# Block 1 of a long convolution: two of four spectra kept as halves, rows 0 and 2 summed first, h loaded in two transfers, new orders

## The chip, the cores and the metric

The kernel runs on one core of one Trainium2 chip. The metric is the device time of one execution in microseconds. Times inside a profile are microseconds from the start of its span.

## The reference

Two layers follow each other, twice over, on x with 2048 positions and 512 channels in bf16. The first is a gated long convolution, the second a feed-forward network (FFN):

```
kv = shift_conv4(k, shift_k) * v
y  = irfft(rfft(pad(kv)) * rfft(pad(ssm_k)))[:2048] + kv * ssm_D
x  = x + layernorm(x) * y
x  = x + (silu(n @ w_gate) * (n @ w_up)) @ w_down     # n = layernorm(x), F = 1792
```

The convolution's y depends on k, v and the filter alone, and not on x; both passes use the same y.

## The kernel before

**Blocks.** The 2048 positions are cut into 4 blocks of 512 (`NB`). A block is held as four rows of 128 positions (position = 4p + r, row r), and its transform has length 1024. The convolution is done block by block: spectra X of kv and G of the filter h, products of X of block i with G of block j summed into Z of block i + j, and one inverse transform for each block of y. The transforms are matmuls with tables of cosines and sines: `fwd`, made on ScalarE from angles, and `inv`, its transpose, made by two DMA transposes (L1158) on SP's queue.

**Spectra of the first block.** All spectra consist of four slots of a real and an imaginary part, 128 partitions by 512 channels each. With a, b, c, d for the partial transforms over two rows each, slot 0 is a + c, slot 2 is a - c, slot 1 is b + d, slot 3 is b - d. `half` (L425) makes partial transforms with two matmuls a part; `butterfly` (L437) adds and subtracts them on VectorE (DVE); `direct` (L450) makes a slot with four matmuls a part and needs no butterfly. Before, G of block 0 is made by `half` and `butterfly`, X of block 0 by `direct` in all four slots. ScalarE (ACT) copies the results out of PSUM (L419), DVE some of them (L422).

**Products and inverse.** `product` (L627) multiplies one slot: two multiplications of 1024 columns (L642) and two combinations of 512 (L646). `inverse_half` (L783) forms z0 + z2, z0 - z2, z1 + z3 and z1 - z3 (L791) and makes each row of y with four matmuls (L797): rows 0 and 2 from the sums, rows 1 and 3 from the differences.

**Units.** The FFN works through units of two rows (a layer, a block, rows 0 and 2 or rows 1 and 3). The first unit takes rows 0 and 2 of block 0. `prologue` (L879) makes its input: DVE multiplies the normalised x with y straight from PSUM (L903, the tile n), adds it to x (L908), takes statistics (L809), GpSimd (POOL) forms rstd (L814), DVE normalises to z (L864), TensorE (PE) transposes z (L920), and a copy by ACT and one by DVE (L925, L923) give zT, from which the first FFN matmuls (L311, tile pf) read. In a unit, gate and up projections fill PSUM, ACT copies them (L970, L974), DVE multiplies them to ht (L977), and the down projection (L990) adds up in the tile pd.

**Loads.** SP issues, in this order: h of block 0 (hn), k of block 0 (kn), v (vt) and x (xc) of block 0, h and v of block 1, the gate weights, the two table transposes, k of block 1, the up and down weights. PE turns h by 16 transposes (L477), k by another 16 (L366), and makes the short convolution with diagonal matrices dg (L1152) in 64 matmuls of 128 columns; `shift_mul` (L497) then multiplies with v on DVE (L524).

**Order.** Every operation is recorded first (`Plan.add`) with its engine, a planned cost, and what it reads and writes. `ORDER` is a written list that gives each recorded operation its place; `Plan.order` sorts by it and assigns buffers from rings, and `Plan.issue` puts out the instructions in that order, so each engine's queue is fixed. Where the plan sees PE idle for more than 0.5 us in the first 32 us, `issue` puts in warming matmuls (tile wm, L1267), whose results nobody reads; their operand wz is set by DVE (L1050).

Of the kernel before, what the change touches and what calls it, by code (L numbers as in the profile page):

```python
# [9 lines left out]
P = 128  # L10
# [22 lines left out]
X0 = 'direct'  # L33
# [9 lines left out]
H_SPLIT = False  # L43
# [7 lines left out]
LASTV = True  # L51
ORDER = [
    0, 8, 122, 2, 4, 5, 12, 9, 3, 6, 1, 31, 32, 33, 10, 14, 7, 11, 15, 16, 18, 21, 17, 20, 22, 23, 36, 30, 56, 73, 153, 24, 40, 25, 41, 34, 42, 38,
    55, 54, 68, 50, 64, 58, 62, 71, 81, 13, 26, 77, 48, 28, 43, 29, 27, 53, 35, 49, 37, 57, 65, 52, 47, 69, 51, 19, 39, 60, 66, 67, 61, 63, 44, 45,
    154, 155, 156, 196, 258, 197, 83, 84, 85, 86, 88, 80, 90, 91, 92, 94, 78, 96, 97, 98, 103, 79, 99, 100, 101, 108, 76, 89, 93, 107, 95, 123, 145,
    171, 147, 176, 159, 87, 82, 114, 115, 121, 105, 111, 113, 102, 104, 46, 59, 70, 75, 72, 74, 118, 109, 106, 110, 112, 116, 117, 126, 131, 136, 140,
    124, 125, 133, 139, 148, 151, 144, 150, 157, 128, 120, 132, 129, 119, 130, 137, 141, 142, 134, 146, 163, 152, 158, 177, 164, 127, 135, 138, 149,
    160, 168, 199, 213, 167, 183, 189, 202, 170, 209, 165, 175, 187, 200, 162, 172, 143, 185, 161, 173, 166, 169, 207, 208, 204, 205, 178, 181, 179,
    180, 225, 226, 182, 184, 206, 212, 234, 192, 215, 186, 198, 190, 193, 195, 194, 201, 210, 211, 216, 217, 227, 230, 233, 221, 228, 235, 237, 229,
    238, 239, 246, 252, 260, 270, 263, 271, 264, 291, 292, 294, 296, 293, 295, 299, 300, 309, 314, 334, 310, 311, 244, 243, 272, 275, 262, 245, 277,  # L60
    276, 203, 222, 232, 188, 214, 218, 174, 191, 219, 236, 254, 285, 257, 281, 320, 321, 231, 241, 223, 224, 273, 286, 315, 317, 305, 307, 289, 301,
    335, 333, 347, 345, 363, 354, 220, 261, 290, 368, 283, 282, 313, 324, 323, 342, 379, 365, 380, 416, 425, 429, 432, 437, 445, 444, 478, 471, 524,
    515, 479, 522, 540, 551, 504, 512, 548, 573, 611, 547, 627, 644, 639, 649, 250, 251, 253, 259, 256, 268, 247, 248, 284, 302, 316, 240, 242, 278,
    279, 269, 274, 280, 288, 306, 322, 327, 266, 298, 249, 255, 287, 297, 265, 267, 318, 331, 328, 308, 319, 312, 325, 330, 336, 338, 337, 339, 340,
    341, 344, 353, 358, 352, 357, 346, 350, 364, 370, 390, 366, 369, 355, 385, 381, 392, 402, 407, 408, 414, 421, 367, 375, 388, 389, 398, 406, 356,
    411, 413, 427, 428, 409, 418, 410, 422, 426, 431, 430, 438, 439, 440, 348, 351, 359, 360, 361, 362, 373, 377, 376, 382, 378, 384, 393, 394, 396,
    395, 397, 401, 404, 412, 420, 446, 417, 443, 441, 452, 451, 453, 454, 466, 483, 482, 486, 487, 488, 499, 492, 497, 500, 507, 510, 527, 508, 536,
    462, 467, 473, 481, 447, 455, 485, 494, 495, 520, 519, 460, 461, 449, 450, 469, 470, 456, 457, 503, 523, 526, 496, 511, 513, 514, 477, 506, 490,
    509, 518, 566, 531, 528, 530, 468, 484, 533, 594, 579, 618, 598, 619, 655, 640, 436, 343, 463, 464, 489, 493, 498, 501, 525, 532, 537, 539, 543,
    538, 541, 544, 546, 559, 564, 567, 572, 304, 400, 383, 475, 476, 491, 505, 549, 574, 586, 587, 591, 589, 601, 608, 614, 660, 672, 675, 729, 332,  # L70
    329, 303, 326, 371, 349, 374, 386, 405, 415, 419, 424, 372, 399, 474, 480, 423, 472, 458, 459, 434, 442, 387, 403, 529, 552, 558, 599, 593, 624,
    669, 648, 542, 535, 502, 433, 517, 516, 521, 448, 569, 534, 545, 575, 560, 576, 435, 465, 555, 581, 582, 595, 606, 609, 628, 625, 631, 641, 643,
    673, 688, 626, 636, 658, 659, 653, 654, 686, 690, 632, 650, 670, 678, 721, 704, 794, 796, 772, 748, 719, 391, 863, 738, 683, 652, 684, 697, 702,
    715, 722, 723, 802, 808, 814, 815, 817, 835, 839, 845, 886, 847, 887, 888, 891, 893, 896, 900, 911, 912, 899, 901, 915, 916, 894, 924, 925, 939,
    941, 950, 957, 955, 958, 972, 979, 1010, 1018, 1044, 565, 570, 580, 588, 577, 583, 578, 590, 592, 613, 621, 561, 568, 550, 556, 553, 563, 554,
    557, 571, 623, 667, 562, 585, 604, 605, 597, 602, 596, 600, 607, 645, 674, 629, 638, 584, 620, 646, 656, 679, 657, 687, 691, 705, 707, 603, 616,
    617, 633, 615, 634, 610, 622, 637, 709, 713, 630, 681, 651, 676, 665, 668, 642, 671, 694, 710, 714, 689, 699, 677, 680, 696, 701, 685, 698, 708,
    717, 716, 693, 700, 682, 692, 706, 718, 724, 720, 725, 726, 730, 731, 737, 739, 761, 762, 752, 755, 785, 798, 792, 734, 767, 768, 769, 758, 759,
    744, 745, 776, 799, 793, 773, 780, 746, 751, 775, 783, 756, 757, 795, 801, 807, 781, 800, 779, 806, 809, 812, 810, 813, 811, 825, 727, 732, 728,
    733, 736, 743, 749, 753, 754, 763, 764, 766, 765, 770, 771, 786, 787, 791, 816, 788, 789, 826, 831, 829, 832, 833, 841, 842, 843, 848, 849, 855,  # L80
    862, 865, 866, 870, 876, 878, 882, 884, 913, 898, 917, 834, 836, 820, 823, 837, 840, 818, 838, 850, 881, 874, 856, 858, 819, 824, 854, 857, 852,
    853, 875, 889, 890, 844, 869, 846, 851, 860, 871, 864, 872, 879, 909, 892, 885, 895, 828, 830, 897, 964, 921, 965, 922, 968, 1013, 1046, 742, 735,
    747, 790, 777, 867, 868, 877, 880, 902, 903, 904, 907, 905, 906, 908, 932, 933, 956, 982, 943, 976, 740, 741, 784, 804, 859, 861, 883, 914, 910,
    937, 945, 974, 961, 981, 990, 996, 998, 1002, 1029, 1030, 1015, 1032, 635, 647, 661, 612, 662, 663, 666, 664, 778, 822, 712, 750, 703, 711, 695,
    760, 805, 821, 774, 782, 797, 803, 827, 873, 993, 992, 1009, 999, 1008, 1006, 1058, 1020, 983, 1024, 971, 1031, 926, 1007, 952, 985, 1036, 967,
    975, 1011, 1052, 1057, 1047, 1056, 1037, 1049, 1060, 1079, 1063, 1106, 1098, 1101, 1135, 1110, 1112, 1109, 1120, 1132, 1137, 1177, 1179, 1161,
    1183, 1182, 1188, 1146, 1147, 1163, 1165, 1192, 1194, 1195, 1212, 1210, 1213, 1108, 1066, 1061, 1069, 1092, 1153, 1157, 1158, 1159, 1214, 1226,
    1235, 1240, 1254, 1247, 1255, 1264, 1265, 1268, 1274, 1273, 1293, 1289, 1279, 1283, 1294, 1320, 1276, 1278, 1305, 1313, 938, 940, 935, 936, 944,
    948, 947, 953, 954, 986, 977, 920, 923, 927, 928, 918, 919, 931, 934, 942, 987, 978, 960, 966, 929, 930, 951, 963, 969, 970, 973, 995, 1005, 946,
    959, 949, 962, 980, 997, 1016, 1035, 1022, 1043, 1072, 1071, 984, 988, 1027, 1028, 1004, 1012, 1014, 1021, 1041, 1054, 1059, 1000, 1019, 989,  # L90
    1001, 1003, 1017, 991, 994, 1025, 1074, 1064, 1040, 1048, 1033, 1045, 1042, 1051, 1023, 1026, 1053, 1075, 1065, 1034, 1038, 1039, 1050, 1055,
    1076, 1067, 1077, 1068, 1083, 1062, 1070, 1073, 1082, 1102, 1113, 1097, 1103, 1124, 1133, 1136, 1090, 1091, 1078, 1080, 1081, 1087, 1086, 1089,
    1096, 1134, 1143, 1114, 1131, 1104, 1105, 1125, 1130, 1095, 1100, 1149, 1150, 1154, 1111, 1115, 1121, 1122, 1140, 1151, 1160, 1156, 1162, 1166,
    1084, 1088, 1085, 1093, 1094, 1099, 1116, 1107, 1117, 1118, 1127, 1128, 1119, 1126, 1129, 1144, 1148, 1152, 1145, 1164, 1168, 1170, 1167, 1169,
    1171, 1172, 1173, 1185, 1190, 1191, 1198, 1200, 1202, 1204, 1206, 1207, 1208, 1220, 1221, 1223, 1236, 1189, 1199, 1181, 1184, 1174, 1176, 1175,
    1196, 1209, 1216, 1218, 1187, 1201, 1186, 1193, 1203, 1205, 1197, 1224, 1225, 1234, 1233, 1217, 1222, 1178, 1180, 1211, 1229, 1215, 1219, 1230,
    1241, 1238, 1227, 1239, 1228, 1237, 1253, 1262, 1277, 1270, 1284, 1329, 1366, 1462, 1123, 1138, 1141, 1142, 1155, 1231, 1232, 1246, 1242, 1258,
    1252, 1297, 1299, 1302, 1303, 1306, 1307, 1308, 1309, 1310, 1312, 1311, 1321, 1139, 1269, 1324, 1325, 1326, 1327, 1334, 1335, 1336, 1338, 1339,
# [140 lines left out]
def kernel(  # L239
# [936 lines left out]
    else:  # L1176
# [22 lines left out]
        elif X0 == "direct":  # L1199
            direct(vt[0], X[0], "pf", eng(XVE[2:]), (2, 1, 3))  # L1200
# [100 lines left out]
```

## Time and profile before

| what | us |
|---|---|
| runs | 344.19, 344.80, 345.65 (median 344.8) |
| the profiled execution, and its span | 344.93, 343.2 |
| busy in the span: PE, DVE, ACT, POOL | 336.4, 283.4, 253.9, 35.3 |
| first matmul; h turned; first matmul of the v spectrum | 1.04; 4.49 to 6.35; 14.62 |
| v products of block 0 on DVE | 12.39 to 15.08 |
| first FFN matmul; end of the last matmul | 33.58; 339.97 |

The profile gives each engine's busy time; PE's matmuls overlap in the record, so the distance from one start to the next tells what one costs. In rows of the timeline the columns are start, duration, engine, source line, operation, tiles written and read, shapes, and in brackets how long the engine was idle before and what ended that.

### The profile page before, as it was taken

To read this page: it belongs to the slowest core of one execution; us is meant where nothing else is said; L and a number is where in the kernel's file an instruction comes from. 1 tells how busy PE (TensorE), PEld (TensorE's weight loads), DVE (VectorE), ACT (ScalarE), POOL (GpSimd) and SP (SyncE) were. 2 spreads that over 40 slices of the span, in tenths; PEclk is the share of its full clock that TensorE was granted. 3 is DMA by queue.
4 is the path that set the end of the run, shared out by engine and by line. 5 is a ranking of instruction groups with operands and counts; after the bars stand their busy time and mean duration, and the time that the engine had idled before them with its cause. 6 is when DMAs were issued, how large, how long until landed. Compare 5 with 4: busy or idle time off the path is not lost.

```text
span 343.2 us, 6553 instructions
## 1 busy us (share of the span) xinstructions
PE 336.4 (98%) x2579; PEld 248.6 (72%) x2610; DVE 283.4 (83%) x482; ACT 253.9 (74%) x504; POOL 35.3 (10%) x46
## 2 busy tenths in 40 slices
PE   8999999999999999999999999999999999999996
PEld 7756868768687676858586777768685877777783
DVE  8899999899999999899999999989998433726022
ACT  6999999899997765958789995779475464446261
POOL 4010100203111000103110100201101001000000
PEclk9999999999999999999999999999999999999999
DMA  7999218310116044040101014210101100110101
GB/s 273 336 316 341 52 27 112 77 32 0 34 31 94 14 95 138 2 94 3 32 2 46 2 46 79 76 32 1 32 0 33 35 13 0 39 39 8 24 26 37
DMA packets 42088, 22.95 MB, mean 67 GB/s; under 512 B 33861, under 2 KB 39882, under 8 KB 42058
## 3 DMA queue, kind: packets, MB, share of 16 engines
q1 hardware_dynamic: 41904, 22.47, 26.6%
q8 instruction: 20, 0.33, 0.4%
q14 instruction: 10, 0.08, 0.1%
q10 hardware_dynamic: 154, 0.07, 0.1%
HBM read 12.33 MB, written 2.10 MB: 42 GB/s over the span
## 4 chain that ended last, share of the span: by engine, by line
PE 91%; ACT 4%; DVE 3%; issue 1%
PE pf L311 54%; PE pd L990 28%; PE ps L311 6%; PE ps L458 1%; ACT H L419 1%; PE wm L1267 1%; DVE bnst L809 1%; ACT hs L487 1%; PE pt L477 1%; ACT X L419 0%; ACT n L859 0%; PE pt L366 0%; DVE m L540 0%; DVE t L665 0%; DVE Z L667 0%
## 5 line engine op out<-in xcount | busy, mean ns | idle before, releaser
L311 PE MATMUL pf<-zT,wu_sb 128*128 128x256 bf16 x896 | 110.4, 273 | 0.1
L311 PE MATMUL pf<-zT,wg_sb 128*128 128x256 bf16 x896 | 110.2, 273 | 0.2
L990 PE MATMUL pd<-wd_sb,ht 128*128 128x512 bf16 (+1 forms) x440 | 102.4, 372 | 1.2
L311 PEld LDWEIGHTS <-wu_sb 128*128 128x128 bf16 x896 | 87.7, 98 | 16.4
L311 PEld LDWEIGHTS <-wg_sb 128*128 128x128 bf16 x896 | 87.6, 98 | 16.5 <-issue 0.8
L974 ACT CAST ht<-pf 128x512 bf16<-128x512 f32 x112 | 64.0, 591 | 29.3 <-PE pf L311 29.1
L970 ACT ACTIVATE sg<-pf 128x512 bf16<-128x512 f32 x112 | 65.5, 603 | 17.4 <-PE pf L311 15.1
L990 PEld LDWEIGHTS <-ht 128*128 128x128 bf16 x462 | 45.2, 98 | 42.5
L977 DVE TENSOR_TENSOR ht<-ht,sg 128x1024 bf16<-128x1024 bf16 (+1 forms) x64 | 39.0, 617 | 24.0 <-ACT sg L970 18.7
L814 POOL TENSOR_TENSOR rstd<-ve,nhalf 128x2 f32<-128x2 f32 x24 | 23.0, 958 | 217.8 <-DVE ve L812 207.6
L1034 ACT CAST dn<-pd 128x512 bf16<-128x512 f32 x30 | 17.0, 589 | 21.0 <-PE pd L990 20.9
L809 DVE BATCH_NORM_STATS2 bnst<-xc 128x6 f32<-128x512 bf16 x48 | 31.6, 684 | 0.6
L419 ACT ACTIVATE X<-ps 128x512 bf16<-128x512 f32 x32 | 19.2, 611 | 4.0 <-PE ps L311 3.4
L653 DVE TENSOR_TENSOR t<-X,G 128x2048 bf16<-128x2048 bf16 x18 | 21.9, 1218 | 0.1
L657 DVE TENSOR_TENSOR t<-X,G 128x2048 bf16<-128x2048 bf16 x18 | 21.9, 1216 | 0.0
L1037 DVE TENSOR_TENSOR xc<-xc,dn 128x1024 bf16<-128x1024 bf16 x15 | 10.3, 689 | 13.4 <-ACT dn L1034 13.2
L665 DVE TENSOR_TENSOR t<-t,t 128x2048 bf16<-128x2048 bf16 x12 | 14.7, 1222 | 0.3
L667 DVE TENSOR_TENSOR Z<-Z,t 128x2048 bf16<-128x2048 bf16 x12 | 14.6, 1220 | 0.2
L840 POOL TENSOR_TENSOR rstd<-ve,nhalf 128x2 f32<-128x2 f32 x8 | 8.7, 1088 | 59.2 <-ACT ve L838 59.1
L419 ACT ACTIVATE H<-ps 128x512 bf16<-128x512 f32 x24 | 13.8, 610 | 0.1
L886 DVE TENSOR_TENSOR n<-n,Yk 128x1024 bf16<-128x1024 bf16 x15 | 10.3, 688 | 4.1 <-ACT n L859 3.8
L604 ACT ACTIVATE kc<-kTb,tapF 128x512 bf16<-128x512 bf16 x16 | 12.1, 783 | 0.0
(105 smaller groups left out, 323.3 us busy)
## 6 DMA issues: line engine op xcount, KB each, us to landing
hn<-in_A_ssm_k_dram SPq DMA_DIRECT2D x4, 512.0 KB, 4.1
vt<-in_A_v_dram SPq DMA_DIRECT2D x4, 512.0 KB, 5.9
xc<-in_A_q_dram SPq DMA_DIRECT2D x4, 512.0 KB, 5.3
out_dram<-xc SPq DMA_DIRECT2D x15, 128.0 KB, 1.8
wg_sb<-in_B_w_gate_dram SPq DMA_DIRECT2D x1, 1792.0 KB
wu_sb<-in_B_w_up_dram SPq DMA_DIRECT2D x1, 1792.0 KB, 8.5
wd_sb<-in_B_w_down_dram SPq DMA_DIRECT2D x1, 1280.0 KB, 12.0
kn<-in_A_k_dram SPq DMA_DIRECT2D x1, 512.0 KB, 4.5
```

Source lines behind the costliest of these rows:

```text
L311: nc.tensor.matmul(o, lhsT=lhsT, rhs=rhs, start=(n == 0), stop=(n == len(terms) - 1))
L419: add("ACT", act(D), lambda: nc.scalar.activation(out=view(), in_=ps.t[:], func=ACT.Copy, scale=scale), r=[ps], w=[(buf, keys)], conv=conv)
L653: dve(n * D, lambda t1=t1, part=part: nc.vector.tensor_mul(out=t1.t[:], in0=x.t[:, sl, 0, :], in1=g.t[:, sl, part, :]), [(x, key(slots, (0 ...
L657: dve(n * D, lambda t2=t2, part=part: nc.vector.tensor_mul(out=t2.t[:], in0=x.t[:, sl, 1, :], in1=g.t[:, sl, 1 - part, :]), [(x, key(slots ...
L665: dve(n * D, lambda t1=t1, t2=t2, comb=comb: nc.vector.tensor_tensor(out=t1.t[:], in0=t1.t[:], in1=t2.t[:], op=comb), [t2], [t1], conv=conv)
L809: add("DVE", 0.6, lambda st=st, i=i: nc.vector.bn_stats(out=st.t[:], in_=xs[c].t[:, i, :]), r=[(xs[c], (i,))], w=[st])
L814: add("POOL", pw, lambda: nc.gpsimd.tensor_tensor(out=rstd.t[:], in0=ve.t[:], in1=nhalf.t[:].to_broadcast((P, n)), op=ALU.pow), r=[ve, nha ...
L970: add("ACT", act(D), lambda ps=ps, o=o, sg=sg: nc.scalar.activation(out=sg.t[:, o:o + 2, :], in_=ps.t[:], func=ACT.Silu), r=[ps], w=[(sg, ...
L974: add("ACT", act(D), lambda ps=ps, o=o, ht=ht: nc.scalar.copy(out=ht.t[:, o:o + 2, :], in_=ps.t[:]), r=[ps], w=[(ht, (o // 2,))], due=(uni ...
L977: dve(n * W, lambda sg=sg, ht=ht: nc.vector.tensor_mul(out=ht.t[:], in0=ht.t[:], in1=sg.t[:]), [sg], [ht], due=(unit, k / pairs, 0.0, "h"))
L990: nc.tensor.matmul((pds[o] if not cs.start else pds[HP]).t[:, cs], lhsT=ht.t[:, q, o * P:(o + 1) * P], rhs=wt["d"].t[:, ft, cs], start=(ft ...
L1034: add("ACT", act(D), lambda o=o: nc.scalar.copy(out=dn.t[:, o, :], in_=pds[o].t[:]), r=[pds[o]], w=[(dn, (o,))], due=(unit, 1.0, 3.0, "h"))
```

## The change

- **h of block 0** is loaded in two transfers of half its channels (`H_SPLIT`), and its 16 transposes become eight groups of two. SP issues the first half, then k, then the second half.
- **X of block 0** is made directly in slots 0 and 2; b and d stay as halves (tile evx), as b and d of the filter do (tile ev). The odd slots of Z get first the products b·b' and d·d' of the halves. Since (b+d)(b'+d') + (b-d)(b'-d') = 2(bb' + dd'), the sum of the odd pair is twice the sum of these products; the factor 2 is put into a second set of tables, `inv2`, which POOL makes in eight operations from `inv`.
- **Rows 0 and 2** are then summed (`inverse_sums`). **Rows 1 and 3** come after the first part of the first unit's prologue (`inverse_differences`): the odd slots 1 of X and G are formed by `butterfly`, multiplied once, and the difference is that product less the sum of the half products.
- The butterflies of the odd slots, for X and for G, move behind the sums; the odd slots' differences are needed by the later blocks only.
- The warming matmuls read a constant of ones in place of wz, and may start at planned time 0.0 in place of 0.3.
- `ORDER` is another list throughout; the flags that assign work to engines are the same. (`VE_D`, "mix" and "mix2" are new options that stay unused.)

```diff
-X0 = 'direct'
+X0 = 'sum1'
-H_SPLIT = False
+H_SPLIT = True
...
+    inv2 = new("dn", "inv2", [P, 8, P], parts=2) if X0 == "sum1" else None
...
+    def doubled():
+        for n, rows in enumerate(((0, 2), (1, 3))):
+            for o in range(4):
+                f, q = DOUBLE[4 * n + o]
+                i = BI[f, q]
+                add("POOL", 0.57, lambda n=n, o=o, i=i: nc.gpsimd.tensor_scalar(
+                    out=inv2.t[:, 4 * n + o], in0=inv.t[:, i, :], scalar1=2.0, scalar2=None, op0=ALU.mult),
+                    r=[(inv, (0 if i < NI else 1,))], w=[(inv2, (n,))])
...
+    def inverse_sums(k):
...
+        doubled()
+        pss = {r: new("pd", "ps", [P, D], F32) for r in (0, 2)}
+        for s in (0, 1):
+            dve(2 * D, lambda s=s: nc.vector.tensor_tensor(
+                out=m.t[:, s], in0=z.t[:, s], in1=z.t[:, s + 2], op=ALU.add), [(z, key((s, s + 2)))], [(m, key((s,)))])
+            turn_part(m, pss, (0, 2), s, s == 0)
...
+    def inverse_differences(k, m, pss):
+
+        z = Z[k]
+        butterfly(ev, G[0], 1, False)
+        butterfly(evx, X[0], 1, False)
+        pss.update({r: new("pf", "ps", [P, D], F32) for r in (1, 3)})
+        dve(2 * D, lambda: nc.vector.tensor_tensor(
+            out=m.t[:, 2], in0=z.t[:, 0], in1=z.t[:, 2], op=ALU.subtract), [(z, key((0, 2)))], [(m, key((2,)))])
+        turn_part(m, pss, (1, 3), 2, True)
+        pair_product(X[0], G[0], z, 1, 1)
+        dve(2 * D, lambda: nc.vector.tensor_tensor(
+            out=m.t[:, 3], in0=z.t[:, 1], in1=m.t[:, 1], op=ALU.subtract), [(z, key((1,))), (m, key((1,)))], [(m, key((3,)))])
+        turn_part(m, pss, (1, 3), 3, False)
+        evacuate_y(k, (1, 3))
...
+        elif X0 == "sum1":
+            evx = spectrum("evx")
+            direct(vt[0], X[0], "pf", eng(XVE[2:4]), (2,))
+            half(vt[0], evx, "bd", 1.0, "pf", eng(XVE[4:]), False)
...
+        if X0 == "sum1":
+            for slot in (1, 3):
+                pair_product(evx, ev, Z[0], slot, slot)
...
-    wz = whole("wz", [P, P])
-    add("DVE", 0.07, lambda: nc.vector.memset(wz.t[:], 0.5), w=[wz], due=-80)
+    ones = nc.const_aps.tensor(1.0, (P, P), BF16)
```

## The prediction

> **What bounds the kernel now.** I read the page first, then the busy time by windows, then the timeline of the first 34 us, then the landing of each early load. On the page TensorE (PE) is the bound:
>
> ```profile
> PE 336.4 (98%) x2579; PEld 248.6 (72%) x2610; DVE 283.4 (83%) x482; ACT 253.9 (74%) x504; POOL 35.3 (10%) x46
> ```
>
> A busy PE need not be at its peak, so I count. The first FFN matmul starts at 33.58, the last matmul of the program ends at 339.97: 306.39 us. In the built program's order stand behind that first one 1792 FFN matmuls of 256 columns (64 in 6.99 us on the chain: 0.109 each), 448.5 of 512 (20 in 4.32: 0.216) and 62 transforms of 512: 195.7 + 96.9 + 13.4 = 306.0 us. PE loses 0.4 us in 306. So **time = start of the first FFN matmul + PE work left behind it + holes + 3.2 us of tail**. The change can win only ahead of 33.58, and any hole behind it costs in full.
>
> How tight the stretch ahead is, the windows say (PE, PEld, DVE, ACT, POOL busy):
>
> ```profile
> 15.40:27.00 11.60, 11.15 (x75) 5.99 (x74) 11.48 (x23) 11.04 (x23) 1.04 (x1) 1.00 1.10 295
> 27.00:33.50 6.50, 6.09 (x71) 4.40 (x71) 6.17 (x17) 6.50 (x15) 0.69 (x1) 1.00 1.18 361
> ```
>
> VectorE (DVE) has 0.12 us idle in 11.6: it carries the path from block 1's product with v to the inverse. The timeline gives the path:
>
> ```profile
> 4.49 1.86 PE L477 MATMUL pt<-ident,hn 128*128 128x128 bf16 x16
> ...
> 6.15 1.06 PE L366 MATMUL pt<-ident,kn 128*128 128x128 bf16 x8
> ...
> 8.87 0.61 PE L366 MATMUL pt<-ident,kn 128*128 128x128 bf16 x8
> ...
> 12.39 2.69 DVE L524 TENSOR_TENSOR vt<-ps,vt 128x512 bf16<-128x512 f32 x4
> ...
> 18.27 1.04 POOL L840 TENSOR_TENSOR rstd<-ve,nhalf 128x2 f32<-128x2 f32 x1 [11.57 <-ACT ve L838]
> ...
> 25.18 1.89 DVE L791 TENSOR_TENSOR m<-Z 128x1024 bf16<-128x1024 bf16 x3
> ...
> 27.00 0.68 DVE L903 TENSOR_TENSOR n<-n,ps 128x512 bf16<-128x512 bf16 x1
> ...
> 31.45 0.73 DVE L864 TENSOR_SCALAR z<-xc,mv,rstd 128x512 bf16<-128x512 bf16 x2
> ```
>
> To be seen: start to start, a transpose takes 0.106 us at 6.15 and 0.056 at 8.87. PE runs at half speed until about 7.4, though the clock column shows 1.00; it had been busy since 1.04 with no idle gap over 0.25.
>
> **Part 1, h in two transfers.** In the changed order SP issues half of h, then k, then the other half. Landings of h, k and v (issued at 0.72, 1.24, 1.77):
>
> ```profile
> DMA to landing us min/median/max: 3.6/3.6/3.6
> ...
> DMA to landing us min/median/max: 4.5/4.5/4.5
> ...
> DMA to landing us min/median/max: 6.1/6.1/6.1
> ```
>
> That is 4.3, 5.74 and 7.87: 512 KB each, one after the other in order of issue, 1.4 to 2.1 us apart. The second half of h is now the end of the first 1024 KB, where k ended: 5.74 instead of 4.3. The first half lands near 3.6 (0.7 less than 4.3). Bounds for the second half: 4.3 (if the halves overtook k) to 5.74; I take 5.74, the row whose bytes it equals. PE turns eight tiles by 4.6, idles to 5.75, turns eight more (0.15 + 8 x 0.106) to 6.75, where it had finished at 6.15: 0.6 late. Behind stand 16 transposes of k (8 x 0.106 + 8 x 0.056), 12 transforms (12 x 0.216) and 64 matmuls of the shift (x 0.056): 7.5 us, with waits 14.3; in the trace the shift ended at 14.2. The last of four v products, 14.39 to 15.08 before, then ends at about 15.2. SP's queue moves by one issue of 0.45; the table transposes wait there behind, but their second landing (about 19) is needed only at 23.
>
> **Part 2, the sums.** Off PE: the odd slots of X directly took 16 matmuls, as halves 8. So 8 x 0.216 = 1.7 us go for good, and four inverse matmuls (0.9) move behind the first FFN matmul: 66 transforms there, 306.9 us in place of 306.0.
>
> DVE ahead of the inverse of rows 0 and 2, by start-to-start of its rows (0.605 for 1024 columns, 0.34 for 512, 0.67 with PSUM). Before, from 15.08: two butterflies of G, eight products, eight combinations, four sums or differences of Z: 14 x 0.605 + 8 x 0.34 = 11.2, and with 0.7 of waits 27.00. After: a wait of 0.4 for the first half spectrum (two v rows, then matmul, ScalarE's copy 0.60), eight products, eight combinations, two sums: 10 x 0.605 + 8 x 0.34 = 8.8, with 0.2 of waits from 15.2 to 24.6. PE's first group of four inverse matmuls ends at 25.1, nine warming matmuls (0.5) stand in the order behind it, the second group ends at 26.5, and DVE can multiply n at 26.7. DVE fills that time with three 0.605 operations, which end at 26.4 and cost nothing.
>
> POOL doubles eight tables; the nearest rows are its dg operations, 0.60 to 0.66. Four must be done before the second inverse group, three of them behind rstd (begins near 22.0, 1.04): 23.05 + 3 x 0.6 = 24.9, hidden if each stays under 0.8. What they cost DVE no row shows directly. Nearest: while POOL made its four dg, DVE's 128-column dg took 0.33 to 0.36 instead of 0.25, so 0.1 for each; upper bound their own 0.6. I take 0.06 each (0.25 for four) since a DVE product is longer than they are. So n is multiplied at 26.95 in place of 27.00. From there the same chain follows (two additions, two statistics, rstd 0.69) less 0.1, as no v product stands in it: z at about 31.3, and the first FFN matmul, behind eight transposes, one transform and 16 shift matmuls as before, at **33.4**: 0.2 won.
>
> **Part 3, what DVE owes later.** Left until after z: a product, two combinations, m3, and the other butterfly half of G and X, 4 x 0.605 + 2 x 0.34 = 3.1 us. In the trace the multiplication of ht from 46.83 to 47.50 feeds the down projection at 47.75: no slack worth the name. Summing DVE's and PE's rows along both orders from z on, the tightest ht stands 0.5 us worse than before in the first 20 us and 1.2 worse near 92 us; there DVE had idled 1.3 us (60 to 90), which it can use up. Bounds 0 to 1.2; I take a hole of 0.4. ScalarE's sums stand as before.
>
> Warming with the constant ones starts PE 0.25 earlier and replaces idling: nothing, save for the clock (below). DVE saves a 0.17 memset that nothing waits for.
>
> **Sum.** -0.2 + 0.9 + 0.4 = +1.1 on the profiled execution's 344.93 (span 343.2): **346.0**. The median of the runs, 344.8, lies 0.13 lower, less than I can tell. Changes within 0.5% (343.1 to 346.5) count as none, about what a measurement of this kernel resolves.
>
> **Rivals.**
> - *The clock comes later (slower).* The new gap, 4.6 to 5.75, cuts the busy run that let the clock rise 6.3 us after 1.04. If the run counts anew from 5.75, full speed comes at 12.05, and half speed from 7.4 on costs (12.05 - 7.4)/2 = 2.3 us of PE, which the shift and v products pass on. Lower bound 0, if such a gap does not count; middle 1.2: 347.2. It decides as soon as the second half lands over a few tenths after the first is turned. For it: half speed did last through 6.3 us of nearly full work. Against: no row shows a gap of 1 us in that time. The Trainium skill (TensorE: Matmul & The Clock Gate, Part 1) says the clock is released after one busy window of about 3.4 us that runs freely; by that, as an estimate, release would fall 3.4 to 6.8 us after 5.75, and the time 0.9 to 2.6 up.
> - *POOL and DVE exclude each other (slower).* If each of four doublings stops DVE for its whole 0.6, the chain loses 2.4 in place of 0.25: 348.2. For it: rstd took 1.04 at 18.27 beside a saturated DVE and 0.69 at 30.62, where DVE was idle. Against: DVE's dg lost 0.1 each, not 0.6. The Trainium skill (SBUF — State Buffer, "SBUF: two separate sides") states such an exclusive lock between GpSimd and a DVE operation with two SBUF inputs; what the trace shows is the smaller loss.
> - *The halves land as wanted.* If the second half is there by 4.9, PE's stretch starts 0.8 earlier, and 346.0 - 0.8 = 345.2, without the hole 344.9. Against: landings in order of issue.
> - *The work removed counts in full.* If DVE's path does not hold PE, 12 x 0.216 = 2.6 us leave the stretch ahead, 0.9 return: 343.2, and below if the gap and idle shrink too. Against: DVE's 0.12 idle.
>
> **Chances.** Forecast 0.42, later clock 0.20, early halves 0.20, full gain 0.10, exclusion 0.08. The range leaves out most of the last two: 343.4 to 348.0. Faster by over 0.5% needs more than the full gain: 0.07. Within: 0.7 of the forecast, nearly all of the early halves, half of the full gain, a little of the clock: 0.55. Slower: 0.38.
>
> **What would show it.** The second half's landing (5.7 or 4.9); the first 0.056 transpose (7.4 or 9 to 12); v products ending at 15.2; n times ps at 26.95; first FFN matmul at 33.4; 66 transforms behind it; idle PE at an ht around 50 or 92 us. A first FFN matmul before 32.5 or holes over 1.2 would make the forecast wrong.

## The result and the profile after

The changed kernel takes 353.72 us (median of six runs, 352.5 to 355.15); the kernel before, in the same rounds, 345.21. The ratio is **1.0257, 95% interval 1.0231 to 1.0284**: slower by 2.6%, and outside the range forecast (343.4 to 348.0). The profiled execution took 353.61, its span is 351.8 (before 343.2): 8.6 us more.

The engines on the page of the changed kernel, and then its windows (PE, PEld, DVE, ACT, POOL busy, the granted clock, DMA share, GB/s):

```profile
PE 337.9 (96%) x2586; PEld 249.0 (71%) x2618; DVE 285.2 (81%) x487; ACT 252.2 (72%) x504; POOL 49.6 (14%) x54
```

```profile
15.40:27.00 11.60, 10.28 (x76) 5.79 (x75) 11.23 (x23) 8.53 (x17) 4.82 (x2) 1.00 1.11 263
27.00:33.50 6.50, 3.98 (x43) 2.74 (x44) 3.21 (x7) 5.31 (x12) 4.14 (x7) 1.00 1.09 357
...
60.00:90.00 30.00, 27.48 (x201) 20.35 (x202) 26.57 (x42) 25.78 (x57) 6.05 (x3) 0.94 0.17 40
72.00:74.00 2.00, 2.00 (x12) 1.40 (x10) 1.93 (x6) 1.83 (x4) 0.00 (x0) 0.52 0.00 0
```

PE's busy time grew by only 1.5; the time is in places where it waits. POOL is busy 14 us longer with eight operations more, although a doubling should take 0.6. Between 27.0 and 33.5 DVE is idle for 3.3 of 6.5 and PE for 2.5; before, it was 0.3 and 0.4. Between 60 and 90 PE stands idle for 2.5, and from 72 to about 75.5 it runs at half the clock.

PE's waits name the two stops:

```profile
PE ps L802 <- POOL inv L793: 2.4, 1, 2.4
PE pf L312 <- ACT sg L1027: 2.4, 1, 2.4
PE pt L480 <- DMA hn<-in_A_ssm_k_dram: 1.8, 2, 1.3
```

The timelines of POOL and of DVE (start, duration) show what stood behind the first:

```profile
19.37 0.74 POOL L793 TENSOR_SCALAR inv<-inv 128x128 bf16<-128x128 bf16 x1 [12.72 <-DMA inv<-fwd]
22.91 5.24 POOL L897 TENSOR_TENSOR rstd<-ve,nhalf 128x2 f32<-128x2 f32 x1 [2.81 <-ACT ve L895]
28.14 3.00 POOL L793 TENSOR_SCALAR inv<-inv 128x128 bf16<-128x128 bf16 x6
```

```profile
16.80 1.29 DVE L741 TENSOR_TENSOR t<-evx,ev 128x1024 bf16<-128x1024 bf16 x2 [0.37 <-ACT evx L422]
...
22.28 1.28 DVE L741 TENSOR_TENSOR t<-evx,ev 128x1024 bf16<-128x1024 bf16 x2
23.48 0.41 DVE L649 TENSOR_TENSOR Z<-t,t 128x512 bf16<-128x512 bf16 x1
...
26.90 0.68 DVE L448 TENSOR_TENSOR X<-evx 128x1024 bf16<-128x1024 bf16 x1
30.64 0.69 DVE L960 TENSOR_TENSOR n<-n,ps 128x512 bf16<-128x512 bf16 x1 [3.06 <-PE ps L802]
...
35.22 0.74 DVE L921 TENSOR_SCALAR z<-xc,mv,rstd 128x512 bf16<-128x512 bf16 x2
```

rstd, two columns of f32, takes 5.24 where it took 0.69 to 1.8 before. It ends at 28.15: 0.57 after DVE's run of operations on SBUF ends (26.90 + 0.68 = 27.58), which has no idle time in it from 16.80 on. (One doubling did get in during that run, at 19.37, asked for when DVE had finished four of its operations.) Behind it in POOL's queue stood the doublings, for them PE's second inverse group, and for rstd ACT's normalised n. So n times ps comes at 30.64 (27.00 before), z at 35.22 (31.45), and the first FFN matmul at 37.52 (33.58).

The same happens once more at 65, in the FFN, where the change has no new work of its own but does have another order:

```profile
65.09 3.61 POOL L897 TENSOR_TENSOR rstd<-ve,nhalf 128x2 f32<-128x2 f32 x1 [13.08 <-ACT ve L895]
```

DVE's run ends at 68.15, rstd at 68.70. ACT had the two normalisations of n ahead of the next gate copy (sg) in its queue, PE ran out of free PSUM and stood idle from 69.0 to 71.44.

Where 8.6 us went, by starts in the two traces: the v products end 1.35 later (16.43, before 15.08); from there to n times ps it takes 14.2 in place of 11.9, **2.3 more**; from there to the first FFN matmul 0.3 more. Behind the first FFN matmul, 311.1 in place of 306.4: the four inverse matmuls 0.9, the hole **2.4**, and about 1.4 of slow clock behind the hole.

### The profile page after: what moved, and what is told of

Same layout as the page of the kernel before. It is cut to its first block, busy times and chain, and to the rows that moved or that the text cites. A ratio compares the mean times of both kernels' runs of the same rounds, so it can differ in the third digit from the quotient of the medians.

```text
span 351.8 us, 6592 instructions
## 1 busy us (share of the span) xinstructions
PE 337.9 (96%) x2586; PEld 249.0 (71%) x2618; DVE 285.2 (81%) x487; ACT 252.2 (72%) x504; POOL 49.6 (14%) x54
## 4 chain that ended last, share of the span: by engine, by line
PE 84%; DVE 6%; DMA 4%; ACT 3%; issue 1%; POOL 1%; SPq 0%; DVEq 0%; POOLq 0%
PE pf L312 50%; PE pd L1047 25%; PE ps L312 5%; DMA wd_sb<-in_B_w_down_dram 3%; DMA hn<-in_A_ssm_k_dram 1%; DVE bnst L862 1%; POOL rstd L897 1%; PE ps L461 1%; DVE ht L1034 1%; DVE m L543 1%; DVE Z L670 1%; PE wm L1343 1%; ACT sg L1027 1%; PE ps L802 0%; ACT jk L887 0%
## 5 line engine op out<-in xcount | busy, mean ns | idle before, releaser
L312 PE MATMUL pf<-zT,wg_sb 128*128 128x256 bf16 x896 | 112.5, 274 | 2.5 <-ACT sg L1027 2.4
L1047 PE MATMUL pd<-wd_sb,ht 128*128 128x512 bf16 (+1 forms) x437 | 100.3, 372 | 1.3
L867 POOL TENSOR_TENSOR rstd<-ve,nhalf 128x2 f32<-128x2 f32 x24 | 26.8, 1116 | 203.0 <-DVE ve L865 203.0
L897 POOL TENSOR_TENSOR rstd<-ve,nhalf 128x2 f32<-128x2 f32 x8 | 14.9, 1865 | 55.2 <-ACT ve L895 55.2
L422 ACT ACTIVATE X<-ps 128x512 bf16<-128x512 f32 x28 | 17.2, 618 | 2.8 <-PE ps L312 1.8
L312 PE MATMUL ps<-hs,fwd 128*128 128x512 bf16 x38 | 13.7, 424 | 1.5 <-ACT hs L490 1.0
```

The costliest lines, as they stand in the source:

```text
L312: nc.tensor.matmul(o, lhsT=lhsT, rhs=rhs, start=(n == 0), stop=(n == len(terms) - 1))
L422: add("ACT", act(D), lambda: nc.scalar.activation(out=view(), in_=ps.t[:], func=ACT.Copy, scale=scale), r=[ps], w=[(buf, keys)], conv=conv)
L867: add("POOL", pw, lambda: nc.gpsimd.tensor_tensor(out=rstd.t[:], in0=ve.t[:], in1=nhalf.t[:].to_broadcast((P, n)), op=ALU.pow), r=[ve, nha ...
L897: add("POOL", PWA, lambda: nc.gpsimd.tensor_tensor(out=rstd.t[:], in0=ve.t[:], in1=nhalf.t[:].to_broadcast((P, n)), op=ALU.pow), r=[ve, nh ...
L1047: nc.tensor.matmul((pds[o] if not cs.start else pds[HP]).t[:, cs], lhsT=ht.t[:, q, o * P:(o + 1) * P], rhs=wt["d"].t[:, ft, cs], start=(ft ...
```

## The experiments

Theory S: POOL is starved while DVE runs operations on SBUF without a break. Rival C: POOL is slow by itself, through the doublings or a switch of its code. Theory H: h in two transfers costs time ahead of the v products. Each kernel is the changed kernel with the edit named; ratios are to the kernel before, run beside it.

**h_first.** The second half of h is issued ahead of k.

```diff
...
+        table[a - 1], table[a + 1] = table[a + 1], table[a - 1]   # a: second half of h in the record, a + 1: k
...
```

> The changed kernel with the second half of h issued ahead of k (the plan then puts eight more warming matmuls before k's transposes); nothing else moves. Theory H (the late half of h and the slower clock behind it cost 1.35 us at the v products): the second half lands near 5.0, k near 6.2, the 512-column matmuls from 7.3 on start 0.216 apart and not 0.43, the v products end at 15.1 to 15.4 in place of 16.43, and the whole falls by 1.0 to 1.3, to about 352.5. Rival: the v products move but the first FFN matmul does not, since rstd on POOL and what stands behind it there set its start: no change, 353.6. If rstd of the first unit (5.24 us) meets VectorE's operations in another phase and gets in early, the fall is larger than 1.3, up to 4.

1.0212 (1.0148 to 1.0276), 349.6 to 354.6. In the profiled execution the v products end at 14.76, and the first rstd takes 1.22 with the first FFN matmul at 32.71; the second takes 3.65 and PE's hole is 2.48. So the first starvation does not come in every execution, and the doublings, all still there, are not enough to cause it.

**no_doublings.**

```diff
-                    pss[r].t[:], lhsT=iT(f, q) if i is None else inv2.t[:, i], rhs=m.t[:, slot, part],
+                    pss[r].t[:], lhsT=iT(f, q), rhs=m.t[:, slot, part],
...
-        doubled()
...
```

> The changed kernel without POOL's eight doublings; the inverse reads the plain tables, so the odd slots' share of rows of block 0 is half of what it should be. rstd stays on POOL. Theory S (POOL is starved by VectorE's unbroken run of operations with two SBUF inputs): rstd at 22.9 still ends 0.55 behind the end of that run, 4 to 5 us long; the inverse's second group no longer waits, n times ps comes at about 29.6 (28.2, then two copies of n on ScalarE), the first FFN matmul at 36.4, the whole about 1.1 lower, 352.5; the second long rstd (3.6 at 65) stays. Rival C (the doublings make rstd slow, by a switch of POOL's code or by holding its queue): rstd takes 0.7 to 1.2, n times ps at 27.5, first FFN matmul at 34.3, the whole 3.2 lower, 350.4.

1.0195 (1.014 to 1.0249). The two rstd in its trace:

```profile
22.97 1.16 POOL L896 TENSOR_TENSOR rstd<-ve,nhalf 128x2 f32<-128x2 f32 x1 [16.14 <-ACT ve L894]
```

```profile
61.51 3.60 POOL L896 TENSOR_TENSOR rstd<-ve,nhalf 128x2 f32<-128x2 f32 x1 [13.00 <-ACT ve L894]
```

Here rival C's numbers were met ahead of the first FFN matmul (n times ps at 27.49, 33.94, the profiled execution 350.06) and theory S's were not. But a kernel with no doubling at all still has the long rstd at 61. By themselves these two runs leave the first place open, since with the doublings it can be short too (h_first). Also, DVE's operation at 22.26 in this trace started 0.02 late, waiting for ACT; rstd got in at the end of the next one, 23.55.

**trains and trains_2.** The disputed thing alone: DVE runs one kind of operation back to back, POOL asks in the middle. From trains_2, the plain kind:

```diff
+            for k in range(COUNT):
+                dst = o[1 + k % 4 if k != at else 0]
...
+                else:
+                    nc.vector.tensor_tensor(out=dst[:, 0:n], in0=a[:, 0:n], in1=b[:, 0:n], op=ALU.mult)
+                if k == at:   # ACT reads what operation k wrote, POOL reads what ACT wrote
+                    nc.scalar.activation(out=jk[:, 0:phase], in_=o[0][:, 0:phase], func=ACT.Copy, scale=1.0)
+                    nc.scalar.activation(out=ve[:], in_=jk[:, 0:2], func=ACT.Copy, scale=1.0)
+                    nc.gpsimd.tensor_tensor(out=rs[:], in0=ve[:], in1=nhalf[:].to_broadcast((P, 2)), op=ALU.pow)
...
```

> Nothing of the reference is computed: 44 short scenes, in each VectorE runs 9 to 14 operations of one kind back to back, and POOL starts one operation beside them, at a phase that a ScalarE copy of 48 to 720 columns sets. Kinds: two SBUF inputs of 1024 or 512 columns; the same, each reading the one before; one SBUF input; one input in PSUM; two inputs with one operation of a single input in the middle. POOL's operation is rstd's (pow, 128x2), in eight scenes a doubling (128x128). Theory S: beside one-input and PSUM operations POOL takes 0.7 to 1.0; beside two-input runs it ends either 0.55 behind the first boundary or, in some phases, 0.55 behind the end of the run (up to 6 us); the single operation in the middle lets it in. Rival C: 0.7 to 1.2 in every scene.

In four of 44 scenes POOL's operation took 3.64 to 3.88 and ended 0.55 after DVE's run; in the rest 0.5 to 1.25. Beside operations that read PSUM it took 0.69 each time. Doublings took 0.54 to 1.06. One of the four starved scenes has operations with a single SBUF input, so it is not the two inputs. All four asked when DVE had finished four operations of the run. Two others that asked then got in, and the rest asked earlier, so the next kernel asks later.

> Nothing of the reference is computed: 72 scenes of 20 operations of VectorE back to back; POOL's rstd (128x2, pow) is released behind VectorE's operation 0, 2, 4, 6, 8 or 10 of the scene, at two or three phases. In the first run of scenes POOL was starved four times in 16 beside operations of 0.34, each time when asked for behind the fifth operation or later, never behind the first three. Theory Q (VectorE holds the port from the time that its queue runs ahead, after some four operations without a wait): starved in nearly all scenes released behind operation 4 to 10, for 512 and 1024 columns alike, and in none behind 0. Rival R (chance at each request): as many starved behind 0 as behind 10. f32 operations of 256 columns and one operation from PSUM in the middle: if POOL gets in there, they open the port; a small f32 copy (tiny) in the middle: open; a pause that waits for rstd: always opens it.

Three scenes from its timeline, released behind operation 2 of 512 columns, behind operation 4 of 1024 (counted from 0), and behind operation 6 of 512 with a copy of one column in the middle. DVE's row is the whole run, POOL's starts when it asks:

```profile
30.36 6.79 DVE L68 TENSOR_TENSOR o<-a,b 128x512 bf16<-128x512 bf16 x20
...
32.16 5.54 POOL L72 TENSOR_TENSOR rs<-ve,nhalf 128x2 f32<-128x2 f32 x1 [6.47 <-DVE o L68]
```

```profile
219.09 12.12 DVE L68 TENSOR_TENSOR o<-a,b 128x1024 bf16<-128x1024 bf16 x20
...
222.89 8.87 POOL L72 TENSOR_TENSOR rs<-ve,nhalf 128x2 f32<-128x2 f32 x1 [12.48 <-ACT ve L71]
```

```profile
467.62 3.77 DVE L68 TENSOR_TENSOR o<-a,b 128x512 bf16<-128x512 bf16 x11
...
470.76 1.18 POOL L72 TENSOR_TENSOR rs<-ve,nhalf 128x2 f32<-128x2 f32 x1 [3.45 <-DVE o L68]
471.31 0.14 DVE L74 COPY jt<-nhalf 128x1 f32<-128x1 f32 x1
471.38 3.10 DVE L68 TENSOR_TENSOR o<-a,b 128x512 bf16<-128x512 bf16 x9
```

In the plain runs POOL got in at the first or second boundary (an end of one operation and start of the next) in nine scenes of nine when DVE had finished at most four operations since its last idle time, and in none of 27 when it had finished five or more: there it waited to the end of the run and then needed 0.55. So in these scenes it is theory Q, and not chance. One SBUF input and f32 starve it alike (12 of 12). A copy of one column opened the port in 12 of 12 and cost DVE 0.07; an operation from PSUM in 6 of 6; a pause in 6 of 6. So a waiting POOL is passed over by one DVE operation after the other, with no doubling near; rival C is out. The Trainium skill (SBUF — State Buffer, "SBUF: two separate sides") has the pair and the lock, which it says the first to start holds "for the whole instruction"; the trace agrees that one excludes the other and that operations from PSUM do not, but here POOL was shut out over as many as 15 ends of operations.

**two_pauses.** A copy that reads rstd, once in each run, so that DVE waits.

```diff
...
+            doors.append((add("DVE", 0.05, lambda: nc.vector.tensor_copy(out=yl.t[:], in_=rstd.t[:]), w=[yl]).n, at))
```

> The changed kernel with two copies of 2 columns added on VectorE that read rstd (one behind the first third of the run at 22.3 to 27.6, one behind the ht operation at 65.2), so that VectorE stands idle until POOL has formed rstd. Theory S: rstd takes about 1.5 at 22.9 (until 24.4) in place of 5.24, and 1.3 at 65.1 in place of 3.61; VectorE loses 0.6 each time; the hole of 2.4 at 69 and the slower clock behind it go (3.8 together); ahead of the first FFN matmul between 0.7 (if the doublings behind rstd are starved in its place until the run ends) and 3.0 is won: 347 to 349. Rival C (POOL is slow by itself): rstd stays at 5.2 and 3.6, VectorE waits all that time in addition, the whole rises to 355 to 358.

1.0111 (1.0065 to 1.0156), profiled execution 345.81: rstd takes 1.23 and 1.38, the hole at 69 is gone, the first FFN matmul comes at 32.92. The median, 348.48, lies in theory S's range, and the runs spread from 345.8 to 349.7. Only the second pause shows what theory S says, though. The first rstd was in before its pause began: it ended at 22.18, so by the 0.55 it got in at 21.63, while DVE stood idle only from 21.93 on, as the rows show:

```profile
20.95 1.23 POOL L897 TENSOR_TENSOR rstd<-ve,nhalf 128x2 f32<-128x2 f32 x1 [2.13 <-ACT ve L895]
```

```profile
21.52 0.41 DVE L649 TENSOR_TENSOR Z<-t,t 128x512 bf16<-128x512 bf16 x1
22.21 0.26 DVE L902 COPY yl<-rstd 128x2 f32<-128x2 f32 x1 [0.28 <-POOL rstd L897]
```

**pauses_h_first, gap_filled, doublings_early.** Further edits on the two pauses: h ahead of k; 14 warming matmuls in the gap between the halves of h; and h ahead of k with three doublings ahead of the first rstd.

```diff
+        doors.append((add("PE", 0.0, lambda: warm("pc", 0, 14)).n, 31.5))
```

```diff
+        table[182], table[183], table[184] = 149.1, 149.2, 149.3
```

> Both edits together: the second half of h issued ahead of k (with eight more warming matmuls before k's transposes), and the two pauses of VectorE. Theory S with H: no rstd over 1.6, no gap over 0.8 ahead of k's transposes, the granted clock stays at 1.00 behind it; first FFN matmul at 32.7 to 33.0, 307.3 of PE work behind it, holes of 0.3: the whole at 344.9 to 346 in every execution, with a spread of about 1 (two pauses alone: 345.8 to 349.7). Rival: the spread of two pauses alone comes from elsewhere (POOL's doublings, starved in some executions): it stays at 3 to 4, the median near 348.

> Two pauses, and 14 warming matmuls between the transposes of the first half of h and those of the second, so that TensorE does not idle for 1.3 to 1.6 there; the second half lands as late as before. Theory K (it is the idle gap that lets the clock fall in some executions, which costs up to 2 us of PE): clock of 1.00 in every execution, no 0.43 between 512-column matmuls, median 345.5 to 346.5. Rival L (the lateness itself costs, or the fall of the clock has another cause): median 348.5 as with two pauses alone, and the fall is seen as often.

> As pauses_h_first, with three of the doublings ahead of the first rstd in POOL's queue (the plan then moves its warming matmuls: eight less at the inverse, nine elsewhere). By theory S these three then meet VectorE's operations with 0.7 each from 18.8 on, are done by 21 in place of 24.7, and the second inverse group no longer waits for them: n times ps at 25.8 to 26.0 in place of 26.3 to 26.5, the first FFN matmul at 32.3, the whole 0.4 to 0.6 below pauses_h_first. Rival: the doublings are no longer late there and something else on VectorE sets n times ps: no difference.

1.0129 (1.0098 to 1.0159), 1.0106 (1.0069 to 1.0143), 1.0122 (1.009 to 1.0154): none clearly better than the pauses alone, the spreads 3.6 to 4.7. For pauses_h_first (348.86, expected 344.9 to 346) the rival was right; gap_filled (347.27) fell between its two theories; doublings_early (348.11) is 0.75 below pauses_h_first, less than the spreads, and its n times ps came at 29.03 in place of 25.8 to 26.0. In the profiled execution of pauses_h_first PE idled 1.1 ahead of k, matmuls of 512 columns then stood 0.43 apart up to 12.5, and the v products ended at 18.41. In doublings_early DVE stood idle 1.17 for rstd, which now had three doublings ahead of it, PE then waited 1.63 for DVE's sum m, and the clock stood at half from 24.5 to 31.4.

**ticks and one_h**, one cause taken away in each, and **one_h_ticks**, both; **one_h_ticks_early** has three doublings ahead of rstd in addition.

```diff
+        for at in (151.5, 163.5, 165.5, 167.5, 168.5, 170.5, 389.5, 390.5):
+            add("DVE", 0.05, lambda: nc.vector.tensor_copy(out=tick.t[:], in_=nhalf.t[:]), w=[tick])   # one column, waits for nothing
...
```

```diff
-H_SPLIT = True
+H_SPLIT = False
...
```

> The changed kernel with eight copies of one column added on VectorE, which wait for nothing: six in the run at 22.3 to 27.6, two beside the operation at 65.2. In the scenes such a copy cost 0.07 and let POOL in each time, at once. Theory S: rstd takes at most 1.3 at 22.9 and 1.1 at 65.1, the doublings follow at 0.5 to 0.7 each, VectorE loses 0.6 in all and never waits for POOL; n times ps 3.2 earlier, at 27.4 or less (given v products at 16.4), the hole of 2.4 near 69 is gone: 346.0 to 348.5, the spread that the clock leaves, at or below two_pauses (348.5). Rival: it was the waiting of VectorE in two_pauses that let POOL in, not the break in the run: rstd stays above 3 in at least one of the two places, 351 to 354.

> The changed kernel with h of block 0 in one transfer and 16 transposes in a row, as before; all else as changed, POOL's rstd and doublings too. Theory H: no idle gap over 0.4 ahead of the v products, full speed from 7.4 on, v products end at 15.1 in every execution. Theory S: the second rstd (65) still takes 3.6 and leaves a hole of 2.4, and the first is starved in some executions: 349 to 352. Rival (the late h was most of the loss): 345 to 346.

> Both undone: h in one transfer and the eight one-column copies. By S with H: v products end at 15.1, n times ps at 26.7 to 27.0, first FFN matmul at 33.3 to 33.6, 306.9 of PE work and 0.3 of holes behind it: 345.0 to 346.0, spread about 1, within 0.5% of before. If a third cause exists beside S and H, it stays above 347.

> As one_h_ticks, with three doublings ahead of the first rstd on POOL. If the second inverse group waits for the doublings there (they ended at 24.9 with h ahead of k), n times ps comes 0.3 to 0.6 earlier, 344.5 to 345.5, level with before (344.6); the rival is that rstd, now behind three doublings, comes too late for the normalised n: n times ps no earlier, 345 to 346.5.

| | h in two transfers | h in one |
|---|---|---|
| plain | 1.0257 (1.0231 to 1.0284) | 1.0150 (1.0100 to 1.0199) |
| with the copies | 1.0068 (1.0039 to 1.0098) | **0.9992 (0.9971 to 1.0014)** |

The copies are worth 1.9% and 1.6%, one transfer 1.1% and 0.8%; together they take away the whole loss. The plain one_h has only four executions, 348.36 to 354.13 (median 350.48, in theory S's range), so of the four figures its is the least certain; the pair with the copies rests on eight and twelve. ticks (347.49) is in theory S's range as well, though its first rstd took 1.62 and n times ps came at 28.12, later than expected. one_h_ticks has a median of 344.25 beside 344.5, below the expected 345.0 to 346.0: its v products ended at 13.59 and not at 15.1. Its timelines of POOL and its window of 60 to 90:

```profile
20.07 1.29 POOL L897 TENSOR_TENSOR rstd<-ve,nhalf 128x2 f32<-128x2 f32 x1 [1.53 <-ACT ve L895]
21.34 3.84 POOL L793 TENSOR_SCALAR inv<-inv 128x128 bf16<-128x128 bf16 x6
```

```profile
59.37 0.77 POOL L897 TENSOR_TENSOR rstd<-ve,nhalf 128x2 f32<-128x2 f32 x1 [12.92 <-ACT ve L895]
```

```profile
60.00:90.00 30.00, 30.00 (x217) 21.03 (x215) 29.82 (x57) 29.84 (x61) 5.46 (x6) 1.00 0.14 35
```

PE does not idle at all from 60 to 90, and from the first FFN matmul (31.80) to the end of the last matmul (338.67) it takes 306.87. In one_h the second rstd took 3.64 and left a hole of 2.46, as expected. Three doublings ahead of rstd gave 1.0027 (1.0007 to 1.0047), 345.22: no gain, and n times ps came 11.83 behind the v products, as in one_h_ticks.

The second rstd, near 60 to 65, is the clean case, since every kernel's trace has it. It took 3.60 to 3.65 in all four kernels without an edit there (after, h_first, no_doublings, one_h), each time with a hole of 2.4 to 2.5; 1.33 to 1.38 in the four with a pause; 0.77 or 0.78 in the five with the copies. None of these nine has a hole over 0.8. The first rstd was passed over to the end of DVE's run in one trace only (after, 5.24), and in gap_filled until the pause let it in; in h_first, no_doublings, one_h, two_pauses and pauses_h_first it took 1.16 to 1.24 and got in ahead of any pause. With the copies it took 0.91 to 1.62. There is one profile of each kernel, so how often the first place is starved is not known.

**ticks_filled and ticks_h_first**: the copies, with h still in two transfers and the gap filled with 14 warming matmuls, or h ahead of k and 18 of them ahead of k's transposes.

> The changed kernel with the eight one-column copies, and 14 warming matmuls between the transposes of the two halves of h (the second half lands as late as in the changed kernel). One transfer of h was worth 3.2 beside the copies (347.5 to 344.3). Theory K (the idle gap of 1.3 to 1.6, which lets the clock fall or rise later, is most of that): a gap under 0.7, no 0.43 between 512-column matmuls behind 8, median 345.0 to 346.0. Theory L (the lateness of the data is most of it, 1.4 or more): 346.5 to 347.5, with v products at 15.8 or later even at full speed.

> The changed kernel with the copies, the second half of h issued ahead of k, and 18 warming matmuls in the gap ahead of k's transposes. h is then turned early, k lands last. Theory K: the gap is filled, so the clock rises as before: v products at 14.5 to 15.2, median 344.3 to 345.3. Theory L: k's late landing costs what the second half's did: 346.5 to 347.5.

1.0072 (1.0051 to 1.0094) and 1.0057 (1.0036 to 1.0077): as with the gap open (1.0068). Of the medians, 346.63 lies in theory L's range and 346.23 between the two; the v products, at 14.84 and 15.04, came earlier than theory L's 15.8 and within theory K's 14.5 to 15.2. The profiled executions say more for K: with a gap of at least 1.0, half speed lasted or came back behind it in four of six (after, no_doublings, ticks, pauses_h_first: v products at 16.40 to 18.41; not in two_pauses and doublings_early: 14.47 and 14.85), with gaps under 0.7 in none of four (h_first, gap_filled and these two: 14.76 to 15.06). With one transfer (one_h_ticks, one_h, one_h_ticks_early) the v products ended at 13.59, 13.99 and 14.46. **How the 0.8 to 1.1% of the two transfers splits between late data and slow clock stays open**; that the split transfer as a whole costs it is shown.

## Why the prediction was wrong

It said 346.0, with a first FFN matmul at 33.4 and holes of 0.4.

- **The step that failed is in part 2**: "Four must be done before the second inverse group, three of them behind rstd (begins near 22.0, 1.04) ... hidden if each stays under 0.8". The doublings took 0.5 to 0.74 in the changed kernel (in others up to 1.06, once 1.45); rstd took 5.24 in place of 1.04. The 1.04 came from a row beside a "saturated DVE" at 18.27, but in the trace of before that run has a break of 0.03 at 18.73, and 0.58 behind it rstd ended. A second row there, 1.79 at 59.97, let one boundary pass and ended 0.55 behind a break at 61.21. I did not ask why the two differ.

  ```profile
  16.74 1.99 DVE L642 TENSOR_TENSOR t<-X,G 128x1024 bf16<-128x1024 bf16 x3
  18.76 0.42 DVE L646 TENSOR_TENSOR Z<-t,t 128x512 bf16<-128x512 bf16 x1
  ```

  ```profile
  59.97 1.79 POOL L840 TENSOR_TENSOR rstd<-ve,nhalf 128x2 f32<-128x2 f32 x1 [12.88 <-ACT ve L838]
  59.99 1.22 DVE L653 TENSOR_TENSOR t<-X,G 128x2048 bf16<-128x2048 bf16 x1
  ...
  61.24 1.23 DVE L665 TENSOR_TENSOR t<-t,t 128x2048 bf16<-128x2048 bf16 x1
  ```

  Both breaks stand where an operation reads the t that the one directly ahead of it wrote. Between the request for rstd and the end of the run, the new order has no such break in either place. So rstd has no fixed price beside DVE: it takes the wait until DVE's run lets it in, and 0.55.
- **The rival on exclusion had the right pair and the wrong victim.** It let POOL stop DVE, 0.6 for each doubling (348.2). DVE lost about 0.1 for each doubling (its 1024 columns took 0.77 in place of 0.68 beside them); it was POOL that lost, by the length of DVE's run. The changed order made such a run, 10.8 us without idle time, and put rstd's request into it.
- **Part 3** put the debt of 3.1 at a hole of 0.4. In one_h_ticks the hole is 0.0 (306.87 behind the first FFN matmul, where the prediction had 306.9 of work) and in ticks 0.1; the seven other kernels with a short second rstd took 307.3 to 309.1, in five of them with a wait of 0.3 to 0.8 for the transposed z. So the 0.4 is neither confirmed nor refuted. The hole of 2.4 at 69 is not DVE's debt: it is rstd again, and behind it came 1.4 of slow clock.
- **Part 1** was mis-sized. The second half of h landed 4.5 after its issue, at 6.22 and not at 5.74, and the first half at 4.30 and not near 3.6 (3.5 to 3.8 in the other kernels with two halves). PE stood idle 1.29, and the clock fell:

```profile
6.27 0.64 PE L480 MATMUL pt<-ident,hn 128*128 128x128 bf16 x8 [1.29 <-DMA hn<-in_A_ssm_k_dram]
...
7.26 1.06 PE L312 MATMUL ps<-hs,fwd 128*128 128x512 bf16 x2
...
9.39 1.64 PE L312 MATMUL ps<-hs,fwd 128*128 128x512 bf16 x4
10.88 0.39 PE L369 MATMUL pt<-ident,kn 128*128 128x128 bf16 x4
```

  The first fence line is the wait for the second half. The four matmuls from 9.39 stand 0.43 apart, transposes at 10.88 0.056. The v products ended 1.35 later, not 0.1: the rival of the later clock, at 0.20, came true as a part of the loss (it had 1.2). The transposes at 4.35 already ran at 0.056, so the clock had come, and was taken back. (A slip in the rival on early halves: without the hole its sum is 344.8, not 344.9.)
- **The early start of the warming was put at nothing.** PE starts at 0.76 in place of 1.04. In the three profiles with one transfer full speed came between 3.4 and 5.5, not at 7.4, and the v products ended at 13.6 to 14.5, not 15.08. No run takes the early start alone, so that this is its doing is not shown.
- **Right**: 66 transforms behind the first FFN matmul (0.9; one_h_ticks took the 306.87 that this makes), and that what is saved ahead would about pay for them: with both causes taken away the change measures as no difference.

## What to carry to other kernels

An operation on GpSimd that the critical path waits for should not be asked for behind the fourth operation of a VectorE run on SBUF without idle time: there it may have to wait for the end of the run, however short it is by itself (0.69). When an edit tightens VectorE's order, look for such runs; a copy of one column in the run (0.07) lets GpSimd in. And of a row that is taken as a price, read what let it end.

## What the runs showed of the hardware

- In the scenes the port is handed over at the first or second boundary when VectorE has finished at most three operations since it last idled. With four finished both were seen (in trains four passed over and two let in, in trains_2 three let in), and with five or more, in trains_2, POOL waits until VectorE idles, reads PSUM, or does a tiny copy. In the kernels the count alone does not tell: in h_first, one_h, two_pauses and pauses_h_first rstd got in more than ten operations into the run. In two_pauses it asked 0.05 ahead of the end of the same operation (L741) as in the changed kernel, where it was passed over. What decided there is open.
- POOL ends 0.55 behind the moment when it gets in; alone it takes 0.69.
- A hole of 2.4 us in PE's work was followed by half speed from 72 to about 75.5 (granted clock 0.52 and 0.63 in windows of 2 us), and the holes of 2.4 to 2.5 in h_first, no_doublings and one_h by as much. Gaps of 1.1 to 1.5 near 6 us were followed by half speed of 3.4 and more in four profiles; gaps of 1.0 and 1.6 in two others were not. The Trainium skill (TensorE: Matmul & The Clock Gate, Part 1) has the clock judged by a free-running window of about 3.4 us; half speed for 3.4 here (granted clock 0.50 from 7.22 to 10.64) agrees, and that like gaps had unlike results does too. In pauses_h_first the clock column says 1.00 where matmuls stand 0.43 apart: the trace's record of the clock begins only at 12.72 there (at 7.28 in the kernel before), and the column counts the time ahead of it as 1.00. Early in an execution the distance of the starts decides.
